# Softmax attention on one core: looped engine programs, another order of the K and V loads, one bank for the output, and a split first load

## The chip, the cores and the metric

The kernel runs on one core of one Trainium2 chip. The metric is the device time of one execution in microseconds. An execution is recorded by the hardware profiler, and "the span" is the time from the first to the last instruction of that record. The core has five engines that run programs of their own: TensorE (PE), VectorE (DVE), ScalarE (ACT), GpSimd (POOL) and SyncE (SP). They wait for each other through semaphores. SP and ACT start transfers, which sixteen DMA engines carry out; each of them has a ring of descriptors for SP's queue, and works through it in order. "The rings" are these sixteen.

## The reference

```python
B, H, Sq, Skv, Dh = 8, 16, 16, 2048, 256        # q: (B,H,Sq,Dh); k, v: (B,H,Skv,Dh); all bfloat16
scale = q.shape[-1] ** -0.5
scores = jnp.einsum('bhqd,bhkd->bhqk', q, k) * scale
attn = softmax(scores, axis=-1)
return jnp.einsum('bhqk,bhkd->bhqd', attn, v)
```

There are 128 heads with 16 queries of 256 elements, and 2048 keys and values each. K and V are 134 MB each, the queries and the output 1 MB each.

## The kernel before, in words

Eight heads make a group, and there are 16 groups (`g`). The tokens of a group lie in two units, `e` = 0 and 1, of four heads each. A unit is 4 MB of K or of V: 128 partitions with 64 consecutive tokens (`T`) of 256 bfloat16 elements. The tile `SL` has four slots of one unit. K of group 0 goes to the slots VA and VB, all later K to KA and KB; V goes to VA and VB, and V of the last group to KA and KB.

**The order of the loads** is the order in which SP issues them: the queries, K 0, K 1, V 0, K 2, V 1, and so on to K 15, V 14, V 15, always unit 0 and then unit 1. A K load waits until QK of the group before has read its slot (`c_qk`), a V load until PV of the group before has read its slot (`c_pv`). K 15's and V 14's second unit are loaded in halves, V 15 in two and eight pieces of falling size, each with a semaphore.

**One group.** DVE transposes each K unit in place in four instructions (line 154), 32x32 blocks of 4-byte pairs. PE computes the scores S = QK for 128 rows (8 heads of 16 queries) and 2048 columns in four PSUM banks: per unit 32 matmuls of 512 columns, in two halves (lines 231 to 247). `QW` holds the queries as weights, zero outside a head's own columns; ACT fills it for the next group behind QK (`qwb`, line 174). DVE takes the negative maximum of each row (line 156), ACT the exponentials in two halves with row sums (line 206), DVE transposes P into `PTc` (line 162) and makes the reciprocal of the sums (lines 164, 166). ACT copies `PTc` into `PTz` with eight copies, four for each unit (line 219), so that each of the 64 tokens of a partition has its own 128x128 weights. PE computes O = PV with 64 matmuls of 256 columns for each unit (line 251), each unit into a PSUM bank of its own, 64 rows of which are used. ACT evicts each half with the factor `rinv` (`evac`, line 180) and issues the store (line 184); `finish(g-1)` stands behind the exponentials of group g and ahead of its copies.

**The programs.** The order on each engine is written out by hand. SP, DVE and ACT have one straight program over all groups. PE has QK 0, a loop over g = 1 to 15 with QK g and PV g-1, and the last PV behind it. The loop's first instruction is set on the first slot of a block of instructions (`head_slot={PE: 0}`). PE's order is therefore QK g, then both halves of PV g-1, and ACT's copies for group g come when PV g-1 is done with `PTz`.

```python
with nc.Fori(1, G, engines=[PE], head_slot={PE: 0}) as g:
    qks(g)
    eng.wait_ge(c_cp, 8 * g)
    for e in range(2):
        eng.wait_ge(s_v[e], 16 * g)
```

Of the kernel before, what the change touches and what calls it, by code (L numbers as in the profile page):

```python
# [7 lines left out]
PE = mybir.EngineType.PE  # L8
BF16 = mybir.dt.bfloat16
F32 = mybir.dt.float32  # L10

T = 64
KA, KB, VA, VB = 0, 1, 2, 3


def bass_standalone__softmax_full_bidir__sampling_kernel(
# [17 lines left out]
    qh = q.rearrange("b h s d -> (b h) (s d)")  # L34
    oh = out.rearrange("b h s d -> (b h s) d")

    with ExitStack() as es:
# [5 lines left out]
        PTc = ec(nc.sbuf_tensor("PTc", [128, T, 32], BF16))  # L43
        PTz = ec(nc.sbuf_tensor("PTz", [128, 2, T, 128], BF16))
        O_fin = ec(nc.sbuf_tensor("O_fin", [128, 2, D], BF16))
        negm = ec(nc.sbuf_tensor("negm", [128, G], F32))
        lsum = ec(nc.sbuf_tensor("lsum", [128, G, 2], F32))
        ltot = ec(nc.sbuf_tensor("ltot", [128, G], F32))
        rinv = ec(nc.sbuf_tensor("rinv", [128, G], F32))

        S_ps = ec(nc.psum_tensor("S_ps", [128, 4, 512], F32))
        O_ps = ec(nc.psum_tensor("O_ps", [128, 4, 512], F32))
# [4 lines left out]
        s_q = sem("s_q")  # L57
        s_k = [sem("s_ka"), sem("s_kb")]
        s_k0 = [sem("s_k0a"), sem("s_k0b")]
        s_v = [sem("s_va"), sem("s_vb")]  # L60
        s_st = [sem("s_st%d" % i) for i in range(2)]
# [4 lines left out]
        c_kt = [[sem("c_kt%d%d" % (e, h)) for h in range(2)] for e in range(2)]  # L66
        c_qk = [sem("c_qka"), sem("c_qkb")]
# [5 lines left out]
        c_pv = [sem("c_pv0"), sem("c_pv1")]  # L73
        c_pl = sem("c_pl")
# [4 lines left out]
        def ap_of(t_ap, offset, dims):  # L79
            return bass.AP(tensor=t_ap.tensor, offset=offset, ap=[list(t_ap.ap[0])] + [list(d) for d in dims])  # L80


        TAIL = [(0, 19), (19, 14), (33, 10), (43, 7), (50, 5), (55, 4), (59, 3), (62, 2)]
        TAIL_A = [(0, 37), (37, 27)]
        s_tail = [sem("s_t%d" % i) for i in range(len(TAIL))]
        s_vl = [sem("s_vl%d" % i) for i in range(len(TAIL_A))]
        s_vc = sem("s_vc")
        s_kl = sem("s_kl")

        def obank(g, e):  # L90
            return e + (2 if g == last else 0)

        def kslot(g, e):
            return (VA, VB)[e] if g == 0 else (KA, KB)[e]
# [4 lines left out]
        def on_sync(eng):  # L99
            eng.dma_start(QT[:], qh).then_inc(s_q, 16)  # L100
            for e in range(2):
                load(eng, ku, 0, e, kslot(0, e), 0, T, s_k0[e])
            for g in range(1, G):
                for e in range(2):
                    if g >= 2:
                        eng.wait_ge(c_qk[e], g)
                    if (g, e) != (last, 1):
                        load(eng, ku, g, e, kslot(g, e), 0, T, s_k[e])
                    else:
                        load(eng, ku, g, e, kslot(g, e), 0, 32, s_k[e])  # L110
                        load(eng, ku, g, e, kslot(g, e), 32, 32, s_kl)
                w = g - 1
                for e in range(2):
                    if w:
                        eng.wait_ge(c_pv[e], w)
                    else:
                        eng.wait_ge(c_qk[e], 1)
                    if (w, e) != (last - 1, 1):
                        load(eng, vu, w, e, (VA, VB)[e], 0, T, s_v[e])
                        if e:  # L120
                            eng.sem_inc(s_vc, 16)
                    else:
                        load(eng, vu, w, e, VB, 0, 32, s_v[e])
                        load(eng, vu, w, e, VB, 32, 32, s_vc)

            eng.wait_ge(c_qk[0], G)
            for (a, n), s in zip(TAIL_A, s_vl):
                load(eng, vu, last, 0, KA, a, n, s)
            eng.wait_ge(c_qk[1], G)
            for (a, n), s in zip(TAIL, s_tail):  # L130
                load(eng, vu, last, 1, KB, a, n, s)
            eng.wait_ge(c_ev, 2 * last + 2)
            eng.dma_start(oh[128 * last:128 * last + 128, :], O_fin[:, last % 2, :]).then_inc(s_fin, 16)
            eng.wait_ge(s_fin, 16)

        def on_gpsimd(eng):
            eng.memset(PTz[:].rearrange("p a t c -> p (a t c)").bitcast(F32), 0.0).then_inc(c_pool, 1)  # L137

        def on_vector(eng):
            eng.memset(QW[:].rearrange("p e m x -> p (e m x)").bitcast(F32), 0.0).then_inc(c_qt, 1)  # L140
            eng.wait_ge(s_q, 16)
            qf = QT[:].bitcast(F32)
            eng.transpose(qf, qf).then_inc(c_qt, 1)  # L143
            for g in range(G):
                for e in range(2):
                    for c in range(4):
                        if g == 0 and c == 0:
                            eng.wait_ge(s_k0[e], 16)
                        elif c == 0:
                            eng.wait_ge(s_k[e], 16 * g)  # L150
                        elif (g, e, c) == (last, 1, 2):
                            eng.wait_ge(s_kl, 16)
                        x = SLf[:, kslot(g, e), 16 * c:16 * c + 16, :].rearrange("p t i -> p (t i)")
                        eng.transpose(x, x).then_inc(c_kt[e][c // 2], 1)  # L154
                eng.wait_ge(c_qk[1], g + 1)
                eng.tensor_reduce(out=negm[:, g:g + 1], in_=S_ps[:].rearrange("p c n -> p (c n)"),  # L156
                                  axis=AX.X, op=ALU.max, negate=True).then_inc(c_mx, 1)
                for h in range(2):
                    eng.wait_ge(c_ex[h], g + 1)
                    if g and h == 0:  # L160
                        eng.wait_ge(c_cp, 8 * g)
                    eng.transpose(PTc[:, 32 * h:32 * h + 32, :].rearrange("p t x -> p (t x)"),  # L162
                                  P_sb[:, 1024 * h:1024 * h + 1024]).then_inc(c_pt, 1)
                eng.tensor_reduce(out=ltot[:, g:g + 1], in_=lsum[:, g, :], axis=AX.X, op=ALU.add).then_inc(c_ri, 1)  # L164
                eng.wait_ge(c_ri, 2 * g + 1)
                eng.reciprocal(rinv[:, g:g + 1], ltot[:, g:g + 1]).then_inc(c_ri, 1)  # L166

        def on_scalar(eng):
            def qwb(g):
                Q, r = g // 4, g % 4  # L170
                for a in range(4):
                    dv = QW[32 * a:32 * a + 32, 0, 16 * a, :]
                    sv = QT[32 * Q:32 * Q + 32, :]
                    eng.activation(ap_of(dv, dv.offset, [[1024 + 512, 2], [2, 64], [1, 2]]),  # L174
                                   ap_of(sv, sv.offset + 2 * (8 * r + a), [[8, 2], [64, 64], [1, 2]]),
                                   ACTF.Copy, scale=scale).then_inc(c_qw, 1)

            def evac(g, e):
                rows = slice(64 * e, 64 * e + 64)
                eng.activation(O_fin[rows, g % 2, :], O_ps[rows, obank(g, e), 0:D],  # L180
                               ACTF.Copy, scale=rinv[rows, g:g + 1]).then_inc(c_ev, 1)

            def store(g):
                eng.dma_start(oh[128 * g:128 * g + 128, :], O_fin[:, g % 2, :]).then_inc(s_st[g % 2], 16)

            def finish(g):
                eng.wait_ge(c_ri, 2 * g + 2)
                if g >= 2:
                    eng.wait_ge(s_st[g % 2], 16 * (g // 2))
                for e in range(2):  # L190
                    eng.wait_ge(c_pv[e], g + 1)
                    evac(g, e)
                eng.wait_ge(c_ev, 2 * g + 2)
                store(g)
# [3 lines left out]
            for g in range(G):  # L198
                if g < last:
                    eng.wait_ge(c_qk[1], g + 1)  # L200
                    qwb(g + 1)
                eng.wait_ge(c_mx, g + 1)
                if g:
                    eng.wait_ge(c_pt, 2 * g)
                for h in range(2):
                    eng.activation(P_sb[:, 1024 * h:1024 * h + 1024],  # L206
                                   S_ps[:, 2 * h:2 * h + 2, :].rearrange("p c n -> p (c n)"), ACTF.Exp,
                                   bias=negm[:, g:g + 1], scale=1.0, accum_out=lsum[:, g, h:h + 1]).then_inc(c_ex[h], 1)
                if 0 < g < last:
                    finish(g - 1)  # L210
                if g == 0:
                    eng.wait_ge(c_pool, 1)
                eng.wait_ge(c_pt, 2 * g + 2)
# [104 lines left out]
```

## Time and profile before

| | |
|---|---|
| median of 3 runs | 636.15 us (636.04 to 636.17) |
| the profiled execution | 636.1 us |
| its span | 634.8 us |
| mean granted TensorE clock | 0.917 |
| busy: PE, DVE, ACT, POOL | 488.3, 365.2, 214.8, 7.1 us |
| DMA | 270.64 MB, 426 GB/s over the span |
| chain that ended last | DMA 58%, PE 23%, DVE 16%, ACT 2% |

The page's DMA row gives the mean busy share of the sixteen rings in forty slices of the span. The timeline gives the start, the duration, the engine and line, what is written and read, and in brackets the idle time before and what ended it; "x8" are eight instructions merged into one row. The windows give for each stretch the busy time and number of instructions of PE, weight loads, DVE, ACT and POOL, then the granted PE clock, the share of the rings and GB/s. A share of the rings a little over 1 comes from packets that overlap.

### The profile page before, as it was taken

How to read it: one execution, taken by the hardware profiler on the slowest of the kernel's cores; microseconds unless marked ns; L12 is line 12 of the kernel's file. 1: busy time of each engine (PE TensorE's matmuls, PEld its weight loads, DVE VectorE, ACT ScalarE, POOL GpSimd, SP SyncE). 2: the span in 40 equal slices, each digit the busy share in tenths (PEclk: the TensorE clock that was granted, in tenths of full speed). 3: DMA queues.
4: the chain of work that ended last, by engine and by line, in shares of the span. 5: the costliest groups of instructions: out<-in, count | busy, mean ns of one | idle time of the engine just before them, and what ended most of it. 6: DMA issues, size and time to landing. Idle time of an engine off the chain costs nothing.

```text
span 634.8 us, 6396 instructions
## 1 busy us (share of the span) xinstructions
PE 488.3 (77%) x3072; PEld 274.9 (43%) x2560; DVE 365.2 (58%) x210; ACT 214.8 (34%) x289; POOL 7.1 (1%) x5
## 2 busy tenths in 40 slices
PE   0738989595896958869597795967959689595998
PEld 0202828154271532716336262452724527144287
DVE  2968583763738546294562945739366393663830
ACT  1042252525035250342513325142252322524170
POOL 4000000000000000000000000000000000000000
PEclk9978999798997989969799797998979989798899
DMA  8999999999999999999999999999999999999997
GB/s 376 436 441 432 428 432 432 430 430 431 432 429 434 429 432 433 429 434 429 433 430 429 432 429 433 430 430 433 434 429 436 433 433 432 432 432 425 430 425 285
DMA packets 13113, 270.64 MB, mean 426 GB/s; under 512 B 1456, under 2 KB 3760, under 8 KB 4400
## 3 DMA queue, kind: packets, MB, share of 16 engines
q1 hardware_dynamic: 10944, 269.55, 98.8%
q10 hardware_dynamic: 2160, 0.98, 0.5%
q8 instruction: 3, 0.05, 0.0%
q14 instruction: 6, 0.05, 0.0%
HBM read 269.48 MB, written 1.05 MB: 426 GB/s over the span
## 4 chain that ended last, share of the span: by engine, by line
DMA 58%; PE 23%; DVE 16%; ACT 2%; issue 0%; SPq 0%
DMA SL<-in_k_dram 58%; DVE SL L154 15%; PE S_ps L234 11%; PE S_ps L235 10%; PE O_ps L251 2%; ACT PTz L219 1%; DVE PTc L162 1%; DVE negm L156 1%; ACT P_sb L206 0%; ACT O_fin L180 0%; SPq L97 0%; SPq L100 0%; DVE rinv L166 0%; DVE ltot L164 0%
## 5 line engine op out<-in xcount | busy, mean ns | idle before, releaser
L154 DVE STREAM_TRANSPOSE SL<-SL 128x2048 f32<-128x2048 f32 x128 | 284.2, 2279 | 157.9 <-DMA SL<-in_k_dram 157.9
L234 PE MATMUL S_ps<-SL,QW 128*128 128x512 bf16 x512 | 214.0, 418 | 143.5 <-DVE SL L154 143.3
L251 PE MATMUL O_ps<-SL,PTz 128*128 128x256 bf16 x2048 | 226.3, 273 | 0.9 <-ACT PTz L219 0.7
L234 PEld LDWEIGHTS S_ps<-SL,QW 128*128 128x128 bf16 x512 | 75.1, 147 | 326.6 <-issue 171.7
L251 PEld LDWEIGHTS O_ps<-SL,PTz 128*128 128x128 bf16 x2048 | 199.8, 98 | 30.9 <-issue 4.5
L235 PE MATMUL S_ps<-SL,QW 128*128 128x512 bf16 x512 | 212.5, 415 | 0.0
L219 ACT ACTIVATE PTz<-PTc 32x1024 bf16<-32x1024 bf16 x128 | 134.9, 1054 | 11.3 <-ACT O_fin L180 5.9
L174 ACT ACTIVATE QW<-QT 32x256 bf16<-32x256 bf16 x64 | 26.8, 419 | 243.3 <-PE S_ps L235 236.2
L156 DVE TENSOR_REDUCE negm<-S_ps 128x1 f32<-128x2048 f32 x16 | 36.7, 2292 | 61.4 <-PE S_ps L235 61.4
L180 ACT ACTIVATE O_fin<-O_ps,rinv 64x256 bf16<-64x256 f32 x32 | 15.0, 468 | 137.6 <-PE O_ps L251 137.5
L162 DVE STREAM_TRANSPOSE PTc<-P_sb 128x1024 bf16<-128x1024 bf16 x32 | 37.9, 1224 | 20.3 <-ACT P_sb L206 20.3
L206 ACT ACTIVATE P_sb<-S_ps,negm 128x1024 bf16<-128x1024 f32 x32 | 35.3, 1109 | 25.5 <-DVE negm L156 25.5
L137 POOL MEMSET PTz<- 128x8192 f32 x1 | 6.9, 6924 | 0.3 <-POOLq L303 0.3
L206 ACT ACTIVATION_READ_ACCUMULATOR P_sb<-S_ps,negm 128x1 f32 x32 | 6.3, 196 | 0.0
L143 DVE STREAM_TRANSPOSE QT<-QT 128x2048 f32<-128x2048 f32 x1 | 2.3, 2312 | 3.7 <-DMA QT<-in_q_dram 3.7
L166 DVE RECIPROCAL rinv<-ltot 128x1 f32<-128x1 f32 x16 | 2.6, 164 | 0.5
L164 DVE TENSOR_REDUCE ltot<-lsum 128x1 f32<-128x2 f32 x16 | 1.8, 112 | 0.0
L174 ACT ACT_TABLE_LOAD x1 | 1.3, 1283 | 0.7 <-PEq L303 0.7
L140 DVE MEMSET QW<- 128x1024 f32 x1 | 0.9, 912 | 1.0 <-PEq L303 1.0
L303 POOL MEMSET const-bfloat16-1.0<- 128x1 bf16 x1 | 0.1, 101 | 0.0
L303 POOL MEMSET const-uint8-127<- 128x1 uint8 x1 | 0.1, 101 | 0.0
L303 POOL MEMSET const-float32-0.0<- 128x1 f32 x1 | 0.1, 98 | 0.2 <-issue 0.2
(1 smaller groups left out, 0.1 us busy)
## 6 DMA issues: line engine op xcount, KB each, us to landing
SL<-in_k_dram SPq DMA_DIRECT2D x31, 4096.0 KB, 25.8
SL<-in_v_dram SPq DMA_DIRECT2D x29, 4096.0 KB, 29.1
SL<-in_k_dram SPq DMA_DIRECT2D x2, 2048.0 KB, 23.7
SL<-in_v_dram SPq DMA_DIRECT2D x2, 2048.0 KB, 29.2
SL<-in_v_dram SPq DMA_DIRECT2D x1, 2368.0 KB, 21.6
SL<-in_v_dram SPq DMA_DIRECT2D x1, 1728.0 KB, 25.4
SL<-in_v_dram SPq DMA_DIRECT2D x1, 1216.0 KB, 20.7
QT<-in_q_dram SPq DMA_DIRECT2D x1, 1024.0 KB, 4.9
```

Of the source, the lines that this page charges most:

```text
L137: eng.memset(PTz[:].rearrange("p a t c -> p (a t c)").bitcast(F32), 0.0).then_inc(c_pool, 1)
L154: eng.transpose(x, x).then_inc(c_kt[e][c // 2], 1)
L156: eng.tensor_reduce(out=negm[:, g:g + 1], in_=S_ps[:].rearrange("p c n -> p (c n)"), axis=AX.X, op=ALU.max, negate=True).then_inc(c_mx, 1)
L162: eng.transpose(PTc[:, 32 * h:32 * h + 32, :].rearrange("p t x -> p (t x)"), P_sb[:, 1024 * h:1024 * h + 1024]).then_inc(c_pt, 1)
L166: eng.reciprocal(rinv[:, g:g + 1], ltot[:, g:g + 1]).then_inc(c_ri, 1)
L174: eng.activation(ap_of(dv, dv.offset, [[1024 + 512, 2], [2, 64], [1, 2]]), ap_of(sv, sv.offset + 2 * (8 * r + a), [[8, 2], [64, 64], [1, 2]]),
L180: eng.activation(O_fin[rows, g % 2, :], O_ps[rows, obank(g, e), 0:D], ACTF.Copy, scale=rinv[rows, g:g + 1]).then_inc(c_ev, 1)
L206: eng.activation(P_sb[:, 1024 * h:1024 * h + 1024], S_ps[:, 2 * h:2 * h + 2, :].rearrange("p c n -> p (c n)"), ACTF.Exp, bias=negm[:, g:g ...
L219: eng.activation(PTz[32 * a:32 * a + 32, z, :, 64 * e + 16 * a:64 * e + 16 * a + 16], sv[:, :, 16 * (a % 2):16 * (a % 2) + 16], ACTF.Copy) ...
L234: return eng.matmul(dst, w, x, start=start, stop=stop)
L235: return eng.add_instruction(mybir.InstMatmult(name=nc.get_next_instruction_name(), engine=PE, start_tensor_calc=start, stop_tensor_calc=stop,
L251: ins = eng.matmul(O_ps[:, bank, 0:D], PTz[:, z, t, :], SL[:, slot, t, :], start=(t == 0), stop=(t == T - 1))
```

## The change

It rewrites the programs of all engines; the arithmetic of the output is the same.

- **Loops.** SP, DVE and ACT run a loop over the groups, with conditional parts for the first and last turns. PE has nested loops for QK 0 and one loop over r = 1 to 17 for all else. `head_slot` is gone. The first QK adds into banks that four matmuls with zero weights have cleared. POOL steps some semaphores up ahead of its memset, so that the first turns find the counts that later turns find.
- **Order.** Turn r on PE is QK r, the second half of PV r-2, then the first half of PV r-1. On SP a turn is K j (both units), the second unit of V j-2, the first unit of V j-1. V 15 goes to VA and VB like all V. The last three V units are loaded in 3, 2 and 8 pieces, each behind a count of PV tokens that have been read (`C` = 16).
- **One bank for O.** Both halves of PV add into one bank of 128 rows, and one eviction of 128 rows takes the place of two of 64. PE waits for it (`c_ev`) before the next group's first half. `O_fin` and `rinv` have a column for every group.
- **ACT.** Copies for unit 1 of group g-1 come in turn g, behind the eviction of group g-2; copies for unit 0 of group g come at the end of turn g. The store is issued behind the copies. DVE waits for the copies of unit 1 before it transposes P.
- **DVE.** K is transposed in two instructions per unit. The first K unit of group 1 is transposed before group 0's maximum.
- **Start.** The queries come in four loads of 32 rows, with another order of heads over partitions. The first five tokens (`FEW`) of K's first unit come in two loads, of 108 and of 20 rows, and the other 59 tokens in one.

```diff
-            eng.dma_start(QT[:], qh).then_inc(s_q, 16)
...
+            def load_v(w, e, a, n):
+                eng.wait_ge(c_pv, 8 * w + 4 * e + (a + n + C - 1) // C)
+                load(eng, vu, w, e, VA + e, a, n, s_p[e][a] if a else s_v[e])
+            for a in range(4):
+                eng.dma_start(QT[32 * a:32 * a + 32, :], qh[a]).then_inc(s_q, 16)
+            for lo, hi in ((0, 108), (108, 128)):
+                eng.dma_start(SL[lo:hi, VA, 0:FEW, :], ku[0, lo:hi, 0:FEW, :]).then_inc(s_k0[0], 16)
+            load(eng, ku, 0, 0, VA, FEW, T - FEW, s_k0[0])
+            load(eng, ku, 0, 1, VB, 0, T, s_k0[1])
...
+            with nc.Fori(2, G, engines=[SP]) as j:
                 for e in range(2):
+                    eng.wait_ge(c_qk, 8 * j + 4 * e - 4)
+                    load(eng, ku, j, e, KA + e, 0, T, s_k[e])
+                jj = eng.to_reg(j)
+                with eng.If_ne(jj, 2):
+                    load_v(j - 2, 1, 0, T)
+                load_v(j - 1, 0, 0, T)
+            for w, e in ((last - 1, 1), (last, 0), (last, 1)):
+                for a, n in PIECES[(w, e)]:
+                    load_v(w, e, a, n)
...
+            with nc.Fori(0, G, engines=[DVE]) as g:
+                eng.wait_ge(c_qk, 8 * g + 8)
...
                 for h in range(2):
                     eng.wait_ge(c_ex[h], g + 1)
-                    if g and h == 0:
-                        eng.wait_ge(c_cp, 8 * g)
+                    if h == 0:
+                        eng.wait_ge(c_cp, 8 * g + 9)
...
+                with eng.If_lt(gg, last):
+                    with eng.If_ne(gg, 0):
+                        eng.wait_ge(s_k[0], 16 * g + 16)
+                        for h in range(2):
+                            kt(0, h, KA)
+                    eng.wait_ge(s_k[1], 16 * g + 16)
+                    for h in range(2):
+                        kt(1, h, KB)
...
+            def evac(n):
+                eng.wait_ge(c_pv, 8 * n)
+                eng.wait_ge(c_ri, 2 * n)
+                eng.activation(O_fin[:, n, :], O_ps[:, 0:D], ACTF.Copy, scale=rinv[:, bass.ds(n, 1)]).then_inc(c_ev, 1)
...
+                with eng.If_ne(g2, 0):
+                    evac(g)
+                    copies(1)
+                    eng.wait_ge(c_ev, g)
+                    eng.dma_start(oh[(g + 14) & 15], O_fin[:, g, :]).then_inc(s_st, 16)
+                with eng.If_lt(gg, G):
+                    eng.wait_ge(c_pt, 2 * g + 2)
+                    eng.wait_ge(c_pv, 8 * g + 4)
+                    copies(0)
...
+            with nc.Fori(1, G + 2, engines=[PE]) as r:
+                rr = eng.to_reg(r)
+                with eng.If_lt(rr, G):
+                    for e in range(2):
+                        for h in range(2):
+                            eng.wait_ge(c_kt, 4 * r + 2 * e + h + 1)
+                            if e + h == 0:
+                                eng.wait_ge(c_ex[1], rr)
+                            ins = qk(e, (2 * h, 2 * h + 1), KA + e)
+                        ins.then_inc(c_qk, 4)
+                with eng.If_ne(rr, 1):
...
+                    eng.wait_ge(c_cp, 8 * r + 1)
+                    eng.wait_ge(s_v[1], 16 * (r - 1))
+                    pv(1, lambda t: lim2 if t in dict(PIECES[(last - 1, 1)]) else lim1)
+                with eng.If_lt(rr, G + 1):
+                    lim = eng.to_reg((r & 16) + 1)
+                    eng.wait_ge(c_ev, rr)
+                    eng.wait_ge(c_cp, 8 * r + 5)
+                    eng.wait_ge(s_v[0], 16 * r)
+                    pv(0, lambda t: lim)
+            eng.wait_ge(s_fin, 16)
```

More of the change, by code (lines that the diff above doesn't have):

```diff
@@ L8 @@
 PE = mybir.EngineType.PE
+ACT = mybir.EngineType.Activation
+DVE = mybir.EngineType.DVE
+SP = mybir.EngineType.SP
 BF16 = mybir.dt.bfloat16
@@ L178, in evac @@
[L178 to L194, printed above, removed]
+                    dv = QW[32 * a:32 * a + 32, :, 16 * a:16 * a + 64, :]
@@ L196, in on_scalar, with copies @@
+            def copies(e):
+                for a in range(4):
+                    rs = 32 * (2 * e + a // 2)
+                    sv = PTc[rs:rs + 32, :, :]
+                    m = 64 * e + 16 * a
+                    eng.activation(PTz[32 * a:32 * a + 32, e, :, m:m + 16],
+                                   sv[:, :, 16 * (a % 2):16 * (a % 2) + 16], ACTF.Copy).then_inc(c_cp, 1)
             eng.wait_ge(c_qt, 2)
             qwb(0)
[L198 to L213, printed above, removed]
[L214 to L220 removed]
@@ new lines, in qk, with pv @@
+                return ins
+            def pv(e, lims):
+                for t in range(T):
+                    if t in s_p[e]:
+                        eng.wait_ge(s_p[e][t], lims(t))
+                    ins = eng.matmul(O_ps[:, 0:D], PTz[:, e, t, :], SL[:, VA + e, t, :],
+                                     start=(e == 0 and t == 0), stop=(e == 1 and t == T - 1))
+                    if t % C == C - 1:
+                        ins.then_inc(c_pv, 1)
+            eng.wait_ge(c_qw, 4)
+            for c in range(4):
+                if c == 0:
+                    eng.wait_ge(c_pool, 1)
+                mm(S_ps[:, c, :], PTz[:, 0, 0, :], PTz[:, 0, 0:4, :].rearrange("p t m -> p (t m)"), True, False, c == 0, False)
```

222 lines of the change are left out of this document (85 added, 137 removed).

## The prediction

> **What bounds the kernel now.** I read the page first, for the engines and the DMA shares, then the last microseconds by windows, then the timeline of one middle group and of the end, then the waits.
>
> ```profile
> span 634.8 us, 6396 instructions
> ...
> PE 488.3 (77%) x3072; PEld 274.9 (43%) x2560; DVE 365.2 (58%) x210; ACT 214.8 (34%) x289; POOL 7.1 (1%) x5
> ...
> DMA  8999999999999999999999999999999999999997
> ...
> q1 hardware_dynamic: 10944, 269.55, 98.8%
> ...
> q8 instruction: 3, 0.05, 0.0%
> q14 instruction: 6, 0.05, 0.0%
> ```
>
> No engine is full, but the DMA is at nine tenths or more in all slices but the first and the last, and the K and V loads (q1) fill 98.8% of it. The same bytes must move after the change. So only four places can change the time: the start before the rings are full, a gap in between, the unevenness with which the sixteen rings finish, and the work behind the last byte. The window view shows the start and one full stretch; the columns after the engines are PE clock, DMA share and GB/s.
>
> ```profile
> 1.70:2.70 1.00, 0.00 (x0) 0.00 (x0) 0.23 (x1) 0.32 (x1) 1.00 (x1) 1.00 0.59 123
> 2.70:5.70 3.00, 0.00 (x0) 0.00 (x0) 0.06 (x1) 0.00 (x0) 3.00 (x1) 1.00 1.14 483
> 5.70:15.40 9.70, 0.00 (x0) 0.00 (x0) 2.31 (x2) 1.65 (x4) 1.95 (x1) 1.00 1.00 432
> ```
>
> At 432 GB/s a unit of 4.19 MB takes 9.7 us. The same view of the end:
>
> ```profile
> 628.00:629.00 1.00, 1.00 (x11) 0.90 (x10) 0.00 (x0) 0.00 (x0) 0.00 (x0) 1.00 1.05 386
> 629.00:630.00 1.00, 1.00 (x11) 0.89 (x10) 0.00 (x0) 0.00 (x0) 0.00 (x0) 1.00 0.56 197
> 630.00:631.00 1.00, 1.00 (x12) 0.90 (x10) 0.00 (x0) 0.00 (x0) 0.00 (x0) 1.00 0.33 119
> 631.00:632.00 1.00, 1.00 (x12) 0.90 (x10) 0.00 (x0) 0.00 (x0) 0.00 (x0) 1.00 0.04 14
> 632.00:633.00 1.00, 0.67 (x7) 0.36 (x4) 0.00 (x0) 0.29 (x1) 0.00 (x0) 1.00 0.00 0
> ```
>
> The rings finish one after another: all busy at 629, half of them for the next microsecond, a third, then almost none. 0.04 of 16 rings in the last one is 0.64 ring-us, so one ring or two run to about 631.3. Level, the 0.56 + 0.33 + 0.04 = 0.93 us behind 629 would be over at 629.93. PE works without a break until after that:
>
> ```profile
> 582.41 17.66 DVE L154 STREAM_TRANSPOSE SL<-SL 128x2048 f32<-128x2048 f32 x8 [10.26 <-DMA SL<-in_k_dram]
> ...
> 618.53 14.15 PE L251 MATMUL O_ps<-SL,PTz 128*128 128x256 bf16 x128 [0.69 <-ACT PTz L219]
> ...
> 632.71 0.47 ACT L180 ACTIVATE O_fin<-O_ps,rinv 64x256 bf16<-64x256 f32 x1 [6.44 <-PE O_ps L251]
> 633.21 0.35 SPq L133 DMA_DIRECT2D out_dram<-O_fin  x1
> ```
>
> The last 128 PV matmuls waited for the copies of the weights (ACT L219), ran 14.15 us and ended at 632.7, some 1.35 us behind the last byte. Behind them lie 2.1 us of eviction and store. So two things lie close to the end: the last ring, and a chain of compute that starts with the last K unit at 582.41.
>
> **The change part by part, against the profiled execution (span 634.8, 636.1 in all, so 1.3 around it; the median of the runs is 636.15, 0.05 above).**
>
> *Start.* SP issues four query loads in place of one, then two short K loads, then the rest of unit 0.
>
> ```profile
> 0.73 6.92 POOL L137 MEMSET PTz<- 128x8192 f32 x1 [0.29 <-POOLq L303]
> 0.74 0.38 SPq L100 DMA_DIRECT2D QT<-in_q_dram  x1
> ...
> 1.17 2.09 SPq L97 DMA_DIRECT2D SL<-in_k_dram  x4
> ...
> 15.34 8.89 DVE L154 STREAM_TRANSPOSE SL<-SL 128x2048 f32<-128x2048 f32 x4 [7.39 <-DMA SL<-in_k_dram]
> ```
>
> An issue took 2.09 / 4 = 0.52 us. A quarter of the queries is 0.26 MB, 0.6 us at 432 GB/s, so SP stays ahead of the rings, and the first issue is where it was. Six issues before the rest of unit 0 (4 + 2) are 3.1 us against 1.0 + 0.33 MB, 3.2 us of data: even. Cost 0; bounds -0.1 to +0.5 (one issue not covered). DVE waits here for the data of unit 0 anyway, and POOL's semaphore steps ahead of its memset have from 7.7 us to the first transposed half at 20 to be made up, before PE's four clearing matmuls need the zeros. The early transpose of group 1's first K unit lies ahead of group 0's maximum: V 0 waits for QK 0, not for the maximum, so no load is held by it; QK 1, and with it the load of K 2, waits for group 0's exponential, near 49 us (35 for K 1's landing, 8.9, 2.3 for the maximum, 2.3 for the exponentials), and is done with its first half by 56, while that load's turn on the rings comes after queries and six units, at 64.
>
> *The skew of the short loads.* A unit has 128 rows of 32 KB, eight per ring, so a row takes 9.7 / 8 = 1.21 us on its ring, and one of five tokens (2.5 KB) 0.095. Even over the rings nothing changes. If the uneven 108 and 20 rows leave some rings without any and give others three more, those are 0.76 us earlier and 0.28 later. I take 0, bounds -0.5 and +0.3. [...]
>
> *Steady state: the chain between two groups.* This is where most is moved. One O bank and two halves: PE does QK g, then the second half of PV g-2, ACT evicts, and PE does the first half of PV g-1. ACT's copies of the second half now come behind that eviction, and DVE must wait for them before it transposes P. Rows of a middle group:
>
> ```profile
> 269.91 8.89 DVE L154 STREAM_TRANSPOSE SL<-SL 128x2048 f32<-128x2048 f32 x4 [10.22 <-DMA SL<-in_k_dram]
> 279.81 8.89 DVE L154 STREAM_TRANSPOSE SL<-SL 128x2048 f32<-128x2048 f32 x4 [1.00 <-DMA SL<-in_k_dram]
> 292.53 2.29 DVE L156 TENSOR_REDUCE negm<-S_ps 128x1 f32<-128x2048 f32 x1 [3.83 <-PE S_ps L235]
> 296.09 2.37 DVE L162 STREAM_TRANSPOSE PTc<-P_sb 128x1024 bf16<-128x1024 bf16 x2 [1.27 <-ACT P_sb L206]
> 298.39 0.11 DVE L164 TENSOR_REDUCE ltot<-lsum 128x1 f32<-128x2 f32 x1
> 298.53 0.17 DVE L166 RECIPROCAL rinv<-ltot 128x1 f32<-128x1 f32 x1
> 308.90 2.31 DVE L154 STREAM_TRANSPOSE SL<-SL 128x2048 f32<-128x2048 f32 x1 [10.20 <-DMA SL<-in_k_dram]
> ...
> L219 ACT ACTIVATE PTz<-PTc 32x1024 bf16<-32x1024 bf16 x128 | 134.9, 1054 | 11.3 <-ACT O_fin L180 5.9
> ```
>
> A period is 308.90 - 269.91 = 39.0 us, four units, and DVE idles 10.2 of it for K. New chain from K's first half at S: its second half lands at S + 9.7 and QK ends 292.53 - 279.81 = 12.7 later, at S + 22.4. Then half of PV 14.15 / 2 = 7.1, eviction 0.5 (one of 128 rows for two of 64; the row is 256 elements long as before, upper bound 0.94), four copies of 1.054 with gaps 4.3, P's transposes 2.4, sum and reciprocal 0.3: S + 37.0. DVE's idle time shrinks from 10.2 to 2.0 us. As the first half takes 8.9 of the 9.7 us before the second lands, another 0.8 is free: 2.8 in all. Transposes twice as long are priced as two old ones. So the steady cost is 0; without that cover each microsecond above 2.8 per group costs some 14 in all.
>
> What must fit into the 2.8 are registers, branches and hand-overs, which no row of before shows on DVE or ACT. The nearest is PE's, which runs a loop already:
>
> ```profile
> PEld O_ps L251 <- issue: 4.5, 15, 0.3
> SPq L97 <- PE S_ps L235: 392.1, 32, 25.8
> SL<-in_k_dram SPq DMA_DIRECT2D x31, 4096.0 KB, 25.8
> SL<-in_v_dram SPq DMA_DIRECT2D x29, 4096.0 KB, 29.1
> ```
>
> 4.5 us over 15 turns, 0.3 each. I take two of these, 0.6, between 0 and 1.5 (five). The loads have more room: a K load is issued 25.8 us before it lands, 16 more than a unit takes. In the new order K's first unit is asked for when QK of its predecessor is done, at S + 8.9 + 3.8 = 12.7 (3.8 is DVE's wait for QK), and its turn on the rings begins at S + 39.0 - 9.7 = 29.3, 17 us later; the V units, asked for behind PV, have 19 or more. No gap, 0. The store moves behind the four copies on ACT, and nothing waits for it before the end.
>
> *Instruction fetches.* The nine instruction packets (q8, q14) share the rings with the data. For one of them:
>
> ```profile
> q8 instruction: 1, 0.02, 2.2%
> ```
>
> That is the DMA view from 37 to 40 us: 2.2% of 16 rings times 3 us is 1.06 us on one ring, which then is late for good, since every load gives each ring the same. Three such and six of half the size, 0.5 at least, are 3.2 + 3.2 = 6.4 ring-us. Of the 0.93 us behind 629 that is 0.4 as a mean, and on single rings 1 to 2 us, which fits the staggered finish. Shorter looped programs should need few of them. Bounds for the last byte: 631.3 (the rings stay uneven) and 629.5 (level, and the fetches gone: 629.93 - 0.4). I take 630.0: near the level end, with 0.5 left because the rings also start unevenly (share 0.59 in the window from 1.7). Gain 1.3.
>
> *The end.* The K units of the last group now come one unit earlier in the order: before V 13's second half. What lands at 582.41 in the row above is the 59th unit, K 15's first half; in the new order the 59th is its second half. So from 582.4, less the 1.3 of levelling, compute runs: QK 12.7, then five halves of PV at 7.1, two evictions with hand-over at 0.6: 49.4, to 630.5. The DMA's own end for the same data is 630.0, and the last piece of two tokens needs its receipt and two matmuls, 0.4 to 1.0, so 630.7. The later one counts: PE ends near 630.8, against 632.7. The pieces of V wait for 16 tokens of PV each: PV 13's second half starts 12.7 us behind K, the ring needs the next V unit at 19.4, and 16 tokens take 1.8: 4.9 us of room, less an issue. Eviction and store keep their 2.1.
>
> *Sum.* Start 0, skew 0, middle 0, end 632.7 to 630.8: -1.9 at most, of which I take 1.75, since both ends of the race are within 0.3 of each other. 636.15 - 1.75 = 634.4.
>
> **The rivals.**
>
> 1. *The rings finish as unevenly as before.* The fetches are not what staggers them, or the loops fetch as often, or the skew lands on the late rings. For it: the rings' share is uneven from the first microseconds. Then the last byte stays near 631.3, PE ends at 631.7 to 632.7, and the time is 635.2 to 636.4, say 635.6. No measurable change, that is within 0.2% (1.27 us), about what a measurement of this kernel can tell from none.
>
> 2. *A loop that fetches its own code again on every turn* (ends slower). Place: the back edge on PE, or on DVE and ACT, which had none. Price: 1.06 us on one ring each time; 15 turns on the same ring make 16 us, 650 us in all; spread over rings, 1 us, which is nothing. It decides from the third repeated fetch on one ring, where the 1.9 us are used up. Against it: PE's loop of before ran 15 turns and q8 shows three packets. For it: that loop has its head placed, and the new ones haven't. [...]
>
> 3. *DVE becomes the bound of a group* (slower). The 2.8 us do not cover branches and hand-overs. At 4 us of them the period is 40.2 and 14 groups cost 17 us: 651. At 3 it is 3 us: 637. Against it: 0.3 is the row, and all of it can be done while the engine waits.
>
> **How the numbers follow.** Forecast 0.62, rival 1 0.20, rival 2 0.09, rival 3 0.09. So faster 0.62, same 0.20, slower 0.18. The likeliest case alone runs from 633.5 (level rings, 0.4 after the last byte) to 634.9 (levelling half done). To hold eight in ten the range reaches over rival 1, and to the first steps of rivals 2 and 3: 633.4 to 636.8.
>
> **What would show it.** Instruction packets: fewer than nine; more than 30 is rival 2. The windows of the last 4 us: shares fall from 1 to 0 within a microsecond; a stair of 3 us is rival 1. DVE's idle time before K's first half: 2 us, not 10; none is rival 3, with a period above 39.0. PE's last matmul within 1 us of the last byte. The prediction is wrong if the DMA share drops below nine tenths in a middle slice, or if the last V pieces are issued late.

## The result, and the profile after

| | before | after |
|---|---|---|
| median of the runs | 636.11 us (635.93 to 636.17) | 638.63 us (637.88 to 639.39) |
| the profiled execution | 636.1 us | 638.84 us |
| its span | 634.8 us | 637.1 us |
| outside the span | 1.3 us | 1.7 us |

The ratio is 1.0039 with a 95% interval of 1.0027 to 1.0050: 2.5 us slower, where 1.75 us faster was forecast, and outside the range. The page of the changed kernel:

```profile
span 637.1 us, 7442 instructions
...
DMA  9999999999999999999999999999999999999997
...
q1 hardware_dynamic: 11142, 269.55, 99.0%
q10 hardware_dynamic: 2160, 0.98, 0.5%
q8 instruction: 1, 0.02, 0.0%
```

The rings are as full as before, 9 in every slice but the last, and nine instruction packets have become one. By these two signs the change did what was forecast. The timeline of DVE from 536 us on shows a late group and the last one (start, duration, and in brackets the idle time before the row):

```profile
536.31 8.77 DVE L145 STREAM_TRANSPOSE SL<-SL 128x4096 f32<-128x4096 f32 x2 [1.89 <-DMA SL<-in_k_dram]
...
570.68 2.37 DVE L164 STREAM_TRANSPOSE PTc<-P_sb 128x1024 bf16<-128x1024 bf16 x2 [9.71 <-ACT PTz L202]
...
575.32 8.77 DVE L145 STREAM_TRANSPOSE SL<-SL 128x4096 f32<-128x4096 f32 x2 [1.92 <-DMA SL<-in_k_dram]
...
585.07 8.77 DVE L145 STREAM_TRANSPOSE SL<-SL 128x4096 f32<-128x4096 f32 x2 [0.98 <-DMA SL<-in_k_dram]
```

The period is 575.32 - 536.31 = 39.0 us as before, and DVE idles 1.9 us ahead of each K, where 2.0 was worked out: the steady state costs nothing. But K 15's second half begins at 585.07, where 582.41 less 1.3 was expected. So the loss lies ahead of the last group, and a steady state with an unchanged period can't hold it. It is there from the start:

```profile
0.75 1.79 SPq L104 DMA_DIRECT2D QT<-in_q_dram  x4
...
7.83 2.31 DVE L141 STREAM_TRANSPOSE QT<-QT 128x2048 f32<-128x2048 f32 x1 [5.89 <-DMA QT<-in_q_dram]
...
18.39 8.77 DVE L145 STREAM_TRANSPOSE SL<-SL 128x4096 f32<-128x4096 f32 x2 [8.25 <-DMA SL<-in_k_dram]
```

DVE gets the first K unit at 18.39 in place of 15.34: 3.05 us late. The windows of the start (PE, weight loads, DVE, ACT and POOL, then PE clock, share of the rings, GB/s) show how:

```profile
1.70:2.70 1.00, 0.00 (x0) 0.00 (x0) 0.24 (x1) 0.32 (x1) 1.00 (x1) 1.00 0.78 213
2.70:5.70 3.00, 0.00 (x0) 0.00 (x0) 0.00 (x0) 0.00 (x0) 3.00 (x1) 1.00 1.08 246
5.70:15.40 9.70, 1.89 (x4) 0.10 (x1) 2.31 (x1) 1.66 (x4) 2.90 (x1) 1.00 1.00 358
```

From 2.7 to 5.7 the rings are busy all the time (share 1.08; before 1.14), and yet they move 246 GB/s in place of 483. SP has issued the four query loads by 2.5 us, so it isn't waited for: the packets themselves take longer. Over the three windows 0.09 MB more, then (483 - 246) x 3 = 0.71 MB and (432 - 358) x 9.7 = 0.72 MB less were moved than before: 1.34 MB, 3.1 us at 432 GB/s. That is the whole delay of K. The end of the changed kernel (before's stands in the prediction):

```profile
632.00:633.00 1.00, 1.00 (x11) 0.71 (x9) 0.00 (x0) 0.00 (x0) 0.00 (x0) 1.00 0.95 349
633.00:634.00 1.00, 1.00 (x10) 0.73 (x9) 0.00 (x0) 0.00 (x0) 0.00 (x0) 1.00 0.18 66
634.00:635.00 1.00, 0.96 (x9) 0.43 (x7) 0.00 (x0) 0.00 (x0) 0.00 (x0) 1.00 0.00 1
```

```profile
635.00 0.47 ACT L195 ACTIVATE O_fin<-O_ps,rinv 128x256 bf16<-128x256 f32 x1 [10.26 <-PE O_ps L255]
```

The stair of shares is shorter, as forecast (0.95, 0.18, 0.00 in place of 1.05, 0.56, 0.33, 0.04). Still the last byte lands near 634.0 in place of 631.3. PE ends at 635.0, 1.0 behind it (before 1.35), so 2.3 later than before; with 0.4 more outside the span this is the 2.7 us of the two profiled executions.

It is not the last byte that PE's end hangs on, though. The chain that ended last (start, duration, what) has its last load in K 15's second half, and only compute behind it:

```profile
558.81 26.24 DMA SL<-in_k_dram
...
597.64 7.00 PE O_ps L255 x64
...
605.57 14.16 PE O_ps L255 x128
...
620.66 14.32 PE O_ps L255 x128
```

From the start of that half's transposes to PE's end it takes 635.0 - 585.07 = 49.9 us. In the runs below that have the new programs it is 49.9 to 50.2, wherever K starts. So what is lost at the start counts at the end by as much as it makes K 15 land later.

### The profile page after: what moved, and what is told of

Same layout as the page of the kernel before. It is cut to its first block, busy times and chain, and to the rows that moved or that the text cites. A ratio compares the mean times of both kernels' runs of the same rounds, so it can differ in the third digit from the quotient of the medians.

```text
span 637.1 us, 7442 instructions
## 1 busy us (share of the span) xinstructions
PE 497.3 (78%) x3076; PEld 274.0 (43%) x2561; DVE 361.2 (57%) x146; ACT 209.0 (33%) x277; POOL 7.1 (1%) x5
## 2 busy tenths in 40 slices
DMA packets 13303, 270.56 MB, mean 425 GB/s; under 512 B 1526, under 2 KB 3830, under 8 KB 4726
## 3 DMA queue, kind: packets, MB, share of 16 engines
HBM read 269.48 MB, written 1.05 MB: 425 GB/s over the span
## 4 chain that ended last, share of the span: by engine, by line
DMA 49%; PE 22%; DVE 13%; issue 12%; ACT 2%; SPq 1%; ACTq 0%; DVEq 0%
DMA SL<-in_k_dram 49%; DVE SL L145 12%; PE O_ps L255 9%; PE S_ps L238 7%; PE S_ps L239 6%; ACT PTz L202 2%; DVE PTc L164 1%; ACT O_fin L195 0%; DVE negm L157 0%; DVEq L155 0%; SPq L104 0%; SPq L95 0%; ACT P_sb L215 0%; ACTq L224 0%; SPq L107 0%
## 5 line engine op out<-in xcount | busy, mean ns | idle before, releaser
L145 DVE STREAM_TRANSPOSE SL<-SL 128x4096 f32<-128x4096 f32 x64 | 280.3, 4422 | 43.4 <-DMA SL<-in_k_dram 42.9
L238 PE MATMUL S_ps<-SL,QW 128*128 128x512 bf16 (+1 forms) x512 | 216.6, 423 | 111.5 <-DVE SL L145 102.5
L255 PE MATMUL O_ps<-SL,PTz 128*128 128x256 bf16 x2048 | 228.7, 273 | 14.1 <-ACT O_fin L195 14.1
L239 PE MATMUL S_ps<-SL,QW 128*128 128x512 bf16 (+1 forms) x512 | 214.8, 420 | 0.0
L238 PEld LDWEIGHTS S_ps<-SL,QW 128*128 128x128 bf16 (+1 forms) x512 | 75.2, 147 | 301.1 <-issue 182.6
L202 ACT ACTIVATE PTz<-PTc 32x1024 bf16<-32x1024 bf16 x128 | 134.9, 1054 | 50.2 <-PE O_ps L255 45.9
L189 ACT ACTIVATE QW<-QT 32x256 bf16 (+1 forms) x68 | 28.5, 420 | 320.5 <-PE S_ps L239 311.1
L195 ACT ACTIVATE O_fin<-O_ps,rinv 128x256 f32 (+1 forms) x16 | 7.6, 473 | 49.1 <-PE O_ps L255 49.1
L238 PE MATMUL S_ps<-PTz 128*128 128x512 bf16 x1 | 0.6, 609 | 12.0 <-ACT QW L189 12.0
L168 DVE RECIPROCAL rinv<-ltot 128x1 f32 x16 | 2.6, 164 | 2.4 <-DVE ltot L166 0.2
L239 PE MATMUL S_ps<-PTz 128*128 128x512 bf16 x3 | 1.5, 634 | 0.0
```

Source lines behind the costliest of these rows:

```text
L145: eng.transpose(x, x).then_inc(c_kt, 1)
L168: eng.reciprocal(rinv[:, bass.ds(g + 2, 1)], ltot[:]).then_inc(c_ri, 1)
L189: eng.activation(dv, sv, ACTF.Copy, scale=scale).then_inc(c_qw, 1)
L195: eng.activation(O_fin[:, n, :], O_ps[:, 0:D], ACTF.Copy, scale=rinv[:, bass.ds(n, 1)]).then_inc(c_ev, 1)
L202: eng.activation(PTz[32 * a:32 * a + 32, e, :, m:m + 16], sv[:, :, 16 * (a % 2):16 * (a % 2) + 16], ACTF.Copy).then_inc(c_cp, 1)
L238: return eng.matmul(dst, w, x, start=start, stop=stop, skip_group_check=not check)
```

## The experiments

The theory: a load whose rows go to 32 neighbouring partitions takes data at about half rate (246 against 483 GB/s in the windows above) while the rings look busy (1.08 against 1.14). The rivals: it is the number of query loads; it is the uneven split of five tokens; it is code fetches; it is something else in the rewritten programs. The kernel before was run beside each of them, with medians from 635.96 to 636.06. "K's start" below is the time at which DVE begins the first K unit.

**One query load.** The changed kernel with the query load of before, all 128 partitions at once. The order of heads over partitions goes back with it, so ACT picks the partitions by four branches.

```diff
-            for a in range(4):
-                eng.dma_start(QT[32 * a:32 * a + 32, :], qh[a]).then_inc(s_q, 16)
+            eng.dma_start(QT[:], qh).then_inc(s_q, 16)
...
+                for Q in range(4):
+                    with eng.If_eq(hi, 4 * Q):
+                        qwq(Q, g & 3)
```

> The changed kernel with its queries in one load of 128 rows, head h on partition h, and four branches on ACT that pick the 32 partitions of a group. Everything else, the split first K unit too, stays. Theory P (a load of 32 partitions goes at half the rate, whatever its count): the ring GB/s from 2.7 to 5.7 us go back from about 200 to above 400, DVE begins the first K unit near 15.9 us in place of 18.4, and the time falls by 2.5 to about 636.1. Theory N (the four loads cost, each for itself): the same 636.1. Theory S (the short K loads of 108 and 20 rows cost the time): it stays near 638.6.

Measured: 636.45 us (11 runs), ratio to before 1.0005 (0.9997 to 1.0014), so 2.2 us under the changed kernel. Window and timeline:

```profile
2.70:5.70 3.00, 0.00 (x0) 0.00 (x0) 0.00 (x0) 0.00 (x0) 3.00 (x1) 1.00 1.06 409
```

```profile
16.06 8.77 DVE L144 STREAM_TRANSPOSE SL<-SL 128x4096 f32<-128x4096 f32 x2 [7.98 <-DMA SL<-in_k_dram]
```

At the same share of the rings 409 GB/s in place of 246, and K 2.3 us earlier. Most of the loss is in the four loads.

**The same four loads in the kernel before**, and nothing else of the change:

```diff
-            eng.dma_start(QT[:], qh).then_inc(s_q, 16)
+            for a in range(4):
+                eng.dma_start(QT[32 * a:32 * a + 32, :], qh[32 * a:32 * a + 32, :]).then_inc(s_q, 16)
```

> The kernel before with one part of the change alone: the queries in four loads of 32 rows. Theories P and N: the first K unit is transposed from 17.8 us on in place of 15.3, and the time rises by 2.5 to 638.6. Theory S: 636.1, no change.

Measured: 637.74, ratio 1.0028 (1.0017 to 1.0039): 1.7 us slower, without loops and without another order.

```profile
2.70:5.70 3.00, 0.00 (x0) 0.00 (x0) 0.00 (x0) 0.00 (x0) 3.00 (x1) 1.00 1.11 249
```

```profile
17.12 8.89 DVE L155 STREAM_TRANSPOSE SL<-SL 128x2048 f32<-128x2048 f32 x4 [7.34 <-DMA SL<-in_k_dram]
```

The same 249 GB/s, and K is 17.12 - 15.34 = 1.78 late. At 249 GB/s 1.05 MB of queries take 4.2 us, at 432 they take 2.4: 1.8. So this one line brings a loss of 1.7 by itself, and its size follows from the rate. The 2.5 that were expected of it were too many: they were the whole loss of the changed kernel.

**Number of loads or partitions.** Four loads again, but each of all 128 partitions with a quarter of the columns; and two loads, of partitions 0 to 63 and 64 to 127. Both keep the order of heads of before.

```diff
+                eng.dma_start(QT[:, 1024 * a:1024 * a + 1024], qh[:, 1024 * a:1024 * a + 1024]).then_inc(s_q, 16)
```

> As the one before, but the queries in four loads again, each of all 128 partitions and a quarter of the columns. Theory P: like one load, 636.1 to 636.4 (rows of 2 KB are a little dearer). Theory N: as the changed kernel, 638.6. Theory S: 638.6.

```diff
+            for a in range(2):
+                eng.dma_start(QT[64 * a:64 * a + 64, :], qh[64 * a:64 * a + 64, :]).then_inc(s_q, 16)
```

> Queries in two loads, of partitions 0 to 63 and 64 to 127. If only the number of rows per load mattered (two per ring in 32, four in 64) half of the loss would be back: 637.4. [...] Theory N (cost per load): 637.2.

Measured: by columns 638.29, ratio 1.0037 (1.0024 to 1.0050); two halves 638.98, ratio 1.0048 (1.0035 to 1.0061). The window of the first, then of the second:

```profile
2.70:5.70 3.00, 0.00 (x0) 0.00 (x0) 0.00 (x0) 0.00 (x0) 3.00 (x1) 1.00 0.78 252
```

```profile
2.70:5.70 3.00, 0.00 (x0) 0.00 (x0) 0.00 (x0) 0.00 (x0) 3.00 (x1) 1.00 1.06 251
```

By columns is a miss: it was to give the time back and didn't. But it loses in another way, for the rings are idle for a fifth of the window (0.78). SP had issued all four by 2.6 us; what leaves the rings idle isn't shown. So this run changed two things and can't decide. The two halves do say something: half as many loads, each of twice as many rows, give nothing back (251 GB/s at a share of 1.06). And since they keep the order of heads of before, that order isn't what costs the time.

**Which partitions.** Two and four loads as before, each with the same rows and bytes, but every second or every fourth partition in place of neighbours:

```diff
+            for a in range(2):
+                eng.dma_start(QT[a:128:2, :], qh[a:128:2, :]).then_inc(s_q, 16)
```

> The run with two query loads of 64 rows again (638.98, split first K unit kept), but the first load takes the even partitions and the second the odd ones, in place of the lower and the upper half. Count of loads, rows per load and bytes are the same. [...]

```diff
+            for a in range(4):
+                eng.dma_start(QT[a:128:4, :], qh[a:128:4, :]).then_inc(s_q, 16)
```

> Four query loads of 32 rows, each taking every fourth partition, in place of 32 neighbours as in the changed kernel (638.63). By partitions: the time nears that of one load, 636.5 to 637, less what four issues of their own cost. By count of loads: 638.6. If four issues cost something for themselves, it stands between this run and the one with two.

Measured: every second 636.91, ratio 1.0011 (1.0002 to 1.0020); every fourth 637.70, ratio 1.0037 (1.0022 to 1.0052). Window and timeline of every second partition:

```profile
2.70:5.70 3.00, 0.00 (x0) 0.00 (x0) 0.00 (x0) 0.00 (x0) 3.00 (x1) 1.00 1.04 385
```

```profile
16.55 8.77 DVE L145 STREAM_TRANSPOSE SL<-SL 128x4096 f32<-128x4096 f32 x2 [8.36 <-DMA SL<-in_k_dram]
```

The same from every fourth:

```profile
2.70:5.70 3.00, 0.00 (x0) 0.00 (x0) 0.00 (x0) 0.00 (x0) 3.00 (x1) 1.00 0.78 270
```

```profile
0.74 2.46 SPq L104 DMA_DIRECT2D QT<-in_q_dram  x4
...
4.22 3.52 SPq L95 DMA_DIRECT2D SL<-in_k_dram  x4
```

Two loads of 64 rows against two loads of 64 rows: 385 GB/s in place of 251, and 2.1 us less, with intervals that don't touch. This decides for the partitions against the number of loads. The loads read other rows of the DRAM as well, but that isn't it: the changed kernel reads every fourth row into neighbouring partitions, the kernel before with four loads reads neighbouring rows, and both come to the same (246 and 249). So neighbours moved 246, 249 and 251 GB/s, whether 32 or 64 of them, and even and odd partitions 385. Why neighbours are slower, no run shows.

Every fourth partition is a miss: 636.5 to 637 was expected. Its median is 0.9 us under the changed kernel's, but the runs overlap (637.34 to 640.62 against 637.88 to 639.39), so no gain is shown. Its rings are idle for a fifth of the window as with the columns, and SP's query issues take 2.46 us in place of 1.79, the K issues 3.52 in place of 1.78. That the issuing side is what is late there is only argued; why it is, stays open. The rate while the rings are busy does follow the partitions: GB/s over the busy share are 270 / 0.78 = 346 here and 252 / 0.78 = 323 by columns (rows of 2 KB), 370 for every second partition, 386 for one load, but 224 to 237 in all runs with neighbours. This is an estimate, since the window holds some K as well.

In these two runs K's start misleads. DVE begins K at 18.68 (every fourth) and 19.34 (columns), later than the changed kernel's 18.39, and yet begins K 15's second half at 583.96 and 584.57, earlier than its 585.07.

**The split of five tokens.** From the kernel with one query load: the first K unit in one load; and the five tokens in one load of 128 rows. Then the uneven split alone in the kernel before.

```diff
-            for lo, hi in ((0, 108), (108, 128)):
-                eng.dma_start(SL[lo:hi, VA, 0:FEW, :], ku[0, lo:hi, 0:FEW, :]).then_inc(s_k0[0], 16)
-            load(eng, ku, 0, 0, VA, FEW, T - FEW, s_k0[0])
+            load(eng, ku, 0, 0, VA, 0, T, s_k0[0])
```

> The kernel with its queries in one load, and the first K unit in one load too (all 128 rows, 64 tokens). In the run with one query load DVE began the first K unit at 16.06 us, against 15.34 in the kernel before, with the same bytes ahead. If the short loads of 108 and 20 rows cost these 0.7 us on all rings: start at 15.35, time 636.45 - 0.7 = 635.75. If they bring something at the end (late rings with less to carry): K starts earlier, but the time stays or rises, 636.5 to 637.

```diff
-            for lo, hi in ((0, 108), (108, 128)):
-                eng.dma_start(SL[lo:hi, VA, 0:FEW, :], ku[0, lo:hi, 0:FEW, :]).then_inc(s_k0[0], 16)
+            load(eng, ku, 0, 0, VA, 0, FEW, s_k0[0])
```

> As the last, but with the five tokens in one short load of 128 rows. If each short load costs, a bit under half of the 0.7 us remains: start at 15.7, 636.1. [...] If the uneven rows bring something at the end: slower than with 108 and 20 rows, above 636.5.

```diff
-            for e in range(2):
-                load(eng, ku, 0, e, kslot(0, e), 0, T, s_k0[e])
+            for lo, hi in ((0, 108), (108, 128)):
+                eng.dma_start(SL[lo:hi, VA, 0:5, :], ku[0, lo:hi, 0:5, :]).then_inc(s_k0[0], 16)
+            load(eng, ku, 0, 0, VA, 5, T - 5, s_k0[0])
```

> The kernel before with the second part alone: its first K unit in loads of 108 and 20 rows for five tokens and one for the rest. If the split costs the start: DVE begins K at 16.0 us in place of 15.34 and the time is 636.04 + 0.7 = 636.7. If it helps the late rings at the end: 635.5 or less. If neither, 636.0.

Measured: one load 635.64 (ratio 0.9994, 0.9985 to 1.0003); one short load 635.96 (1.0000, 0.9991 to 1.0009); the split in the kernel before 636.91 (1.0013, 1.0004 to 1.0022), 0.85 slower. The start of K in the kernel with one load:

```profile
15.32 8.77 DVE L142 STREAM_TRANSPOSE SL<-SL 128x4096 f32<-128x4096 f32 x2 [7.38 <-DMA SL<-in_k_dram]
```

That is before's 15.34 again. With one short load it is 15.63, with the two uneven ones 16.06, so 0.3 for a short load and 0.4 more for the uneven pair; the medians follow (635.64, 635.96, 636.45). The two steps are small against the scatter of the runs (635.43 to 636.93 with one short load); their sum is clear in both kernels, for with the split alone the kernel before begins K at 16.26, 0.92 late. The split levels nothing at the end that would pay for it.

**PE's last wait.** The kernel with one query load and the first K unit in one load, without `eng.wait_ge(s_fin, 16)` at the end of PE's program, which SP has too:

```diff
-            eng.wait_ge(s_fin, 16)
```

> The kernel with one query load and one first K load, less PE's last wait (for the final store). The changed kernel's time lies 1.7 to 1.9 us above its span, the kernel before's 1.2 to 1.3. If PE's last wait puts its closing code behind the store and so lengthens the execution behind the span: the difference falls to 1.3 and the time by 0.4 to 635.35. If the difference comes from something else: no change from the run with the wait.

Measured: 635.42, ratio to before 0.9990 (0.9981 to 0.9999), the best of all but the next, and faster than both kernels. Against the run with the wait it is 0.22 less, and the difference is where it was looked for: outside the span lie 1.52 to 1.66 us in all 11 runs with the wait, 1.28 to 1.36 in all 11 without (before 1.26 to 1.39). Its end:

```profile
582.08 8.77 DVE L142 STREAM_TRANSPOSE SL<-SL 128x4096 f32<-128x4096 f32 x2 [0.97 <-DMA SL<-in_k_dram]
```

```profile
629.00:630.00 1.00, 1.00 (x11) 0.70 (x9) 0.00 (x0) 0.00 (x0) 0.00 (x0) 1.00 0.89 321
630.00:631.00 1.00, 1.00 (x10) 0.74 (x9) 0.00 (x0) 0.00 (x0) 0.00 (x0) 1.00 0.07 25
631.00:632.00 1.00, 0.98 (x9) 0.43 (x7) 0.00 (x0) 0.00 (x0) 0.00 (x0) 1.00 0.01 2
632.00:633.00 1.00, 0.00 (x0) 0.00 (x0) 0.00 (x0) 0.47 (x1) 0.00 (x0) 1.00 0.00 0
```

The share of 0.07 from 630 on is 1.1 ring-us of 16, so by this estimate one ring alone runs on to about 631, a microsecond behind the rest, and PE ends with it at 632.0.

**The one late ring.** In the changed kernel and in this one a single instruction packet of q8 comes some 65 us into the span, among the K and V loads, far behind the delay at the start. (This one also has one packet of q14, of half the size.) The DMA view of the changed kernel from 62 to 70 us:

```profile
q8 instruction: 1, 0.02, 0.8%
```

0.8% of 16 rings times 8 us is 1.02 us on one ring. To move it ahead of the data, QK 0 was put into PE's loop as its turn 0, behind the rest of the body, so that PE passes over all its code at once (the base is the kernel without the last wait):

```diff
-            with nc.Fori(1, G + 2, engines=[PE]) as r:
+            with nc.Fori(0, G + 2, engines=[PE]) as r:
...
+                with eng.If_eq(rr, 0):
+                    first()
```

> The kernel with one query load, one first K load and without PE's last wait (635.42), with QK 0 moved behind the rest of the body in PE's loop, as its turn 0. PE so jumps over its whole program before the first data move, and the 16 KB instruction packet that came at 63 us comes at about 1 us. If that one packet makes the last ring late (in the trace one ring ends 1.1 us behind the mean of the sixteen): no q8 packet behind 10 us, the last K unit is there 1.1 us earlier, and the time is 634.4. If another ring is as late, or the end hangs on compute: 635.4 as before.

Measured: 635.36, ratio 0.9989 (0.9980 to 0.9998); no difference to 635.42. The end of it:

```profile
630.00:631.00 1.00, 1.00 (x10) 0.66 (x9) 0.00 (x0) 0.00 (x0) 0.00 (x0) 1.00 0.17 64
631.00:632.00 1.00, 1.00 (x11) 0.67 (x9) 0.00 (x0) 0.00 (x0) 0.00 (x0) 1.00 0.03 9
```

A miss for the time: the packet did come early, within the first 8 us of the record, but not ahead of the data. What it costs can be read from DVE's K rows, first of the base, then of this run:

```profile
15.45 8.77 DVE L142 STREAM_TRANSPOSE SL<-SL 128x4096 f32<-128x4096 f32 x2 [7.43 <-DMA SL<-in_k_dram]
```

```profile
16.73 8.77 DVE L142 STREAM_TRANSPOSE SL<-SL 128x4096 f32<-128x4096 f32 x2 [7.40 <-DMA SL<-in_k_dram]
...
582.04 8.77 DVE L142 STREAM_TRANSPOSE SL<-SL 128x4096 f32<-128x4096 f32 x2 [0.97 <-DMA SL<-in_k_dram]
```

The first K unit begins 1.28 us later than in the base, and DVE's transpose of the queries ahead of it 1.31 (7.02 against 5.71). For the last group, when the base has long had its packet too, both run alike (572.30 against 572.34 for the first half of K 15, 582.04 against 582.08 for the second). So one packet costs K 1.3 us, which by these rows are still there at the last unit, and moving it from between 60 and 66 us to the first 8 changes nothing at the end. By the 49.9 above, PE would end near 582.08 - 1.28 + 49.9 = 630.7 without the packet. That is an estimate from these rows and holds if no other ring is as late; no run has it.

## Why the prediction was wrong

The measured difference is +2.5 us against -1.75. From the runs it falls into four parts, each a difference of two medians, as the kernels above were undone one after another:

| part | predicted | measured |
|---|---|---|
| four query loads of 32 partitions | 0 | 638.63 - 636.45 = +2.2 |
| five tokens in 108 and 20 rows | 0 | 636.45 - 635.64 = +0.8 |
| PE's last wait | not in the sum | 635.64 - 635.42 = +0.2 |
| loops, order, one bank, fetches, end | -1.75 | 635.42 - 636.06 = -0.6 |

- **Start: the step that failed.** It priced a quarter of the queries at "0.6 us at 432 GB/s" and looked only at whether SP stays ahead of the rings. SP did stay ahead. What was taken over without a row is the rate: 432 was measured on loads of 128 partitions, and loads of 32 neighbours ran at 246. The bounds (-0.1 to +0.5) held an issue that isn't covered and none for the rate. Of the 2.2 us 1.7 come back when the loads are put alone into the kernel before; the other 0.5 appear only beside the split and the new programs, and weren't taken apart.
- **The skew of the short loads.** 0 was taken, with +0.3 as the upper bound; it cost 0.8. The bounds counted only which ring carries how many rows, and no run shows the rings without rows, or with three more, that they were worked out for. The page of the changed kernel has 1526 packets under 512 B for 96 issues, ten fewer than 16 for each, where the kernel before has 1456 = 91 x 16; how the rows lie on the single rings, no view shows. What the runs showed is a later landing of the unit: 0.3 at K's start for one short load of all 128 rows, which was not in the bounds, and 0.4 more for the uneven pair.
- **Steady state: right.** The period of 39.0 and the idle time of 1.9 against 2.0 bear out the chain through one bank, two halves and the copies, with their hand-overs. Rival 3 (DVE as the bound) didn't come.
- **Instruction fetches: fewer, as forecast, the gain mis-sized.** One packet in place of nine, and rival 2 (a fetch on every turn) didn't come. The stair got shorter in the changed kernel (with one query load it is still 1.03, 0.55, 0.04 from 629 on), but of the 1.3 that K 15's second half was to land earlier, the kernel without the three losses has 0.3 (582.08 against 582.41). The one packet of q8 that is left costs K 1.3 by the rows above; the step had the number for it (1.06 us on one ring) and still took the level end plus 0.5. It also moved K 15 by what the last byte was to win, though one of before's q8 packets comes only at 628 us (4.6% of 16 rings from 628 to 629.5 us), 46 us behind K 15. And the six packets of q14 were priced at 0.5 at least; in before's DMA view each is 1.9 to 2.1% of 16 rings in its microsecond, 0.3, so all nine are 5.1 ring-us and not 6.4.
- **The end: right but for half a microsecond.** From K 15's second half to the end of PE it took 49.9 against 49.4. For the 0.4 to 1.0 behind the last piece the prediction had no row, and no run shows it; PE ends 1.0 behind the last byte, but by its own chain, and its last 128 matmuls take 14.32 against before's 14.15, so little of it is waiting for pieces. The -0.6 of the table's last row shows in the profiled executions as 0.3 from K 15's landing and 0.4 from this chain (49.9, where before takes 632.7 - 582.41 = 50.3 from its 59th unit to PE's end). Rival 1 (rings as uneven as before) had the time of the kernel without the three losses nearly right, 635.6 against 635.42, by luck: it had the last byte hold PE's end.
- **Around the span** 1.3 was taken over unchanged; it was 1.7 to 1.9 in the changed kernel's runs. PE's wait for the last store brings some 0.3 of that (1.52 to 1.66 with it, 1.28 to 1.36 without); the rest stays open. A wait that is added at the end of a program was not priced.

No rival had a slower start. The three that were worked out looked at the end and at the middle, where the diff is largest; the loss lay in a few of its smallest lines. So the measured time fits none of them.

## What to carry to other kernels

A rate taken from one shape of load holds for that shape (here 432 GB/s for 128 partitions, 246 for 32 neighbours): when a load is cut, ask which partitions each piece reaches, and read GB/s beside the busy share, since busy rings at half the GB/s look full (share 1.08 at 246 GB/s, 1.14 at 483). This kernel is bound by the DMA from start to end (q1 99.0% of the rings), and what the rings failed to move in the first fifteen microseconds was lost in the whole: the first K unit 3.05 us later, the 59th unit 2.66 (585.07 against 582.41). So a cut at the start has to earn what it costs there. A levelling gain goes by the latest ring: with two of nine instruction packets left in the kernel without the three losses, the 59th unit landed only 0.3 earlier (582.08 against 582.41). And ask which load the last chain of compute hangs on: here it was the last K unit, 50 us ahead of the end, and not the last byte.

## What was not expected of the hardware

- Loads of 32 or 64 neighbouring partitions moved 246 to 251 GB/s with a busy share of 1.06 to 1.11; even and odd partitions, the same rows and bytes, 385 at 1.04; all 128 in one load 381 to 483 at 0.98 to 1.14, the lowest with the five tokens split in the kernel before.
- Query loads in four pieces with 2 KB rows, or in every fourth partition, left the rings a fifth idle (0.78) from 2.7 to 5.7 us.
- One more engine that waits for the last store cost 0.2 us, outside the span (1.52 to 1.66 us there with the wait, 1.28 to 1.36 without).
- The changed kernel, with loops on four engines, had a single instruction packet in the whole span, 1.02 us on its ring. In the kernel without the three losses K began 1.28 us later with such a packet in the first 8 us than with one between 60 and 66 us, and at the end both began K 15's second half alike (582.04 and 582.08): its 1.3 us were still there more than 500 us behind it.
